# Two experts' weights, one group's keys and a held-back transpose: reordering the loads of a fused attention and mixture-of-experts kernel

## The chip, the cores and the metric

The kernel runs on one core of one Trainium2 chip. The metric is device time in microseconds (us), from launch to the end of the last store; lower is better. A core has a matrix engine (TensorE, "PE" in the profile, its weight loads "PEld"), VectorE (DVE), ScalarE (ACT), GpSimd (POOL) and SyncE (SP). Each engine runs its own instruction stream in order and waits on semaphores. SP issues transfers only; POOL both computes and issues the transfers that cast from fp32 to fp16. Sixteen DMA engines serve all queues.

## The reference

Attention over 4 batches, 8 heads, 768 positions and 64 channels. Three heads (0, 2, 6) use plain causal attention; the five others see only the first 4 positions and a window of 64. The result, 3072 tokens of 512 channels, goes through four experts; every expert sees every token, and their outputs are summed with normalised weights.

```python
scores = scale * np.matmul(q, k.transpose(0, 1, 3, 2))
causal = rel >= 0
stream_keep = causal & (is_sink | in_win)
scores = np.where(mask[None, :, :, :], scores, -1000000000.0)
a = np.exp(scores - np.max(scores, axis=-1, keepdims=True))
attn = np.matmul(a / (np.sum(a, axis=-1, keepdims=True) + 1e-09), v)

x = attn.transpose(0, 2, 1, 3).reshape(3072, 512)
p = domain_probs / (domain_probs.sum(-1, keepdims=True) + 1e-09)
for e in range(4):
    h = np.maximum(x @ w1[e], 0.0)          # 512 -> 1024
    out += p[:, e:e + 1] * (h @ w2[e])      # 1024 -> 512
```

## The kernel before

**Groups.** The tokens are cut into 8 groups of 384 (half a batch each). `attention(b, c)` computes group g = 2b + c into a tile `xT[g]`, channels on partitions. The experts work through tokens in three stages: `plain_steps(0, 3, e, ...)` for each expert e on all of group 0 (three tiles of 128 tokens), `plain_steps(3, 1, e, ...)` on the first tile of group 1, and then `pair_steps` on ten pairs of tiles. Group 0's attention runs alone at the start (`front`, driven by the hand-written string `FRONT`). All later attention is woven into the expert work.

**The weave.** `moe_steps` yields after each few matmuls, with a modelled length and a share; the loop at the end adds them up in `spent` and calls `attention_step` while the planned attention is behind what `due` says. For group 1 `due` interpolates in `FIRST` (L1746): pairs of (expert work done, in units of one expert on group 0; fraction of group 1's attention to be done by then). A unit's layer 1 is weighed with 0.6 and its layer 2 with 1.4. So FIRST decides where in the instruction streams of PE, DVE and ACT group 1's attention stands.

**One unit.** In `plain_steps` layer 1 takes 8 blocks of four matmuls of 384 columns (L1224), each emptied by ACT with a ReLU (L1251). For expert e the first 7, 4, 2 or 2 blocks start with the first half of the contraction (channel tiles 1 and 0, in chunk 0 of w1(e)) and come back for the second half (chunk 2). Layer 2 (L1269) takes six runs of four matmuls of 512 columns, in the order first half of tiles 0 and 1, second half of tiles 0 and 1, tile 2; DVE adds each finished tile to the accumulator (L1286).

**Group 1's attention.** It has no DMA transpose for its inputs: keys and queries arrive as rows (`k16`, `qt16`, by `load_triples`) and `transposes(hp)` turns a pair of heads on PE (L792), the queries into one PSUM buffer, the keys into another. For hp of 0 and 1 both come from `pV`, which has two buffers, and for 2 and 3 from `pA`, which has four and serves scores and layer 1 too. ACT empties the queries (L805, hp below 2), DVE the keys of the even head (L813) and of the odd one (L825). Then `scores(h)` (L893) fills a `pA` bank by tile, ACT takes the exponential (L911), DVE masks (L918, L922), `values` follows (L951 for the three plain heads, L1003 for the others). The plain heads' outputs go to `x_one` (head 0) and `x_pair` (heads 2 and 6), and SP turns each by one DMA transpose into `xT[g]` (L985).

**The loads.** From L575 to L602 POOL's stream holds by hand the casts of the early values, the memsets and the requests for all weights and for group 1's keys, queries and values. w1(e) is four requests (chunk 0 and 2, each for two halves u of the partitions), w2(e) two. `landed(x)` is a copy of one element by POOL into `seen`: POOL waits there until the transfer that wrote x is done. Each POOL request also takes one of eight semaphores in turn, so it waits until the eighth request before it has landed. The early keys, queries and values of group 0 come on the queues of SP and ACT (L454, L437, L439) in fp32, to `k32`, `q32` and `v32`.

Of the kernel before, what the change touches and what calls it, by code (L numbers as in the profile page):

```python
# [12 lines left out]
FP16 = mybir.dt.float16  # L13
# [6 lines left out]
def kernel(  # L20
# [33 lines left out]
    nc = tc.nc  # L54
    P = 128
    B, H, S, D = q.shape
    E, DM, F = moe_w1.shape
# [3 lines left out]
    HP = H // 2  # L61
# [10 lines left out]
    SH = [h for h in range(H) if not RETR[h]]  # L72
# [15 lines left out]
    pers = ctx.enter_context(tc.tile_pool(name="pers", bufs=1))  # L88
# [53 lines left out]
    bS = early[:, 1792:2272].rearrange("p (t x) -> p t x", t=3)  # L142
    eps = pers.tile([P, 1], FP32, name="eps")
    seen = pers.tile([P, 1], FP16, name="seen")[0:1, :]
    mC = pers.tile([P, P], FP16, name="mC")
    mS = pers.tile([P, 4, TQ], FP16, name="mS")
    mW = mS.rearrange("p t x -> p (t x)")[:, 0 : (WT + 2) * WQ].rearrange(
# [22 lines left out]
    def half(u):  # L170
        return slice(u * D, (u + 1) * D)
# [5 lines left out]
    def own_v(h):  # L177
        return half(PLACE[h][1])
# [10 lines left out]
    def v_tiles(b, c, h):  # L189

        if RETR[h]:
            return vR[b % 2][:, 3 * c : 3 * c + 3, RH.index(h), :]
        if b:
            return windows(vSf)[:, :, SH.index(h), :]
        return vS[:, c, :, SH.index(h), :]
# [10 lines left out]
    def rows_of(x, b, h, c):  # L206
        return x[b, h, c * CH : (c + 1) * CH, :].rearrange("(j p) d -> p j d", p=P)

    def tiles_of(x, b, h, c):
        return x[b, h, c * CH : (c + 1) * CH, :].rearrange("(t r) d -> r t d", r=TK)  # L210

    def windows_of(x, b, h, c):

        assert b > 0
        first = ((b * H + h) * S + c * CH - WO) * D
        return bass.AP(x.tensor, x.offset + first, [[D, P], [WQ * D, WT], [1, D]])
# [85 lines left out]
    def load_v(b, c, heads):  # L302
        for h in heads:
            t = v_tiles(b, c, h)
            if RETR[h]:
                gp.dma_start(out=t[:, :, 0:D], in_=rows_of(v, b, h, c))
            elif b:
                gp.dma_start(  # L308
                    out=t[:, :, own_v(h)], in_=windows_of(v, b, h, c)
                )  # L310
            else:
                gp.dma_start(
                    out=t[R0:P, :, own_v(h)],
                    in_=tiles_of(v, b, h, c),
                )
# [7 lines left out]
                out=vS[0:NS, c, t, :, :], in_=vS[R0 : R0 + NS, 0, 0, :, :]  # L323
            )

    def load_w1(e, chunks=(0, 2)):
        x = moe_w1[e].rearrange("(u c d) f -> u d c f", u=2, c=DMP)
        for c in chunks:
            for u in range(2):
                gp.dma_start(  # L330
                    out=w1sb[half(u), e * DMP + c : e * DMP + c + 2, :],
                    in_=x[u, :, c : c + 2, :],
                )

    def in_pairs(e):

        return e < 2
# [11 lines left out]
    def load_w2(e):  # L349
        x = w2sb[:, e * FTP : (e + 1) * FTP, :]  # L350
        for n in range(2):
            if in_pairs(e):
                m = slice(n * FTP // 4, (n + 1) * FTP // 4)
                gp.dma_start(
                    out=x.rearrange("p (m j) d -> p m (j d)", j=2)[:, m, :],
                    in_=moe_w2[e].rearrange("(m p j) d -> p m (j d)", p=P, j=2)[
                        :, m, :
                    ],
                )
                continue  # L360
            m = slice(n * FTP // 2, (n + 1) * FTP // 2)
            gp.dma_start(
                out=x[:, m, :],
                in_=moe_w2[e].rearrange("(fo fi) d -> fi fo d", fi=P)[:, m, :],
            )
# [44 lines left out]
    def rows32(n):  # L410
        x = hA[:, n * 6 * H * D : (n + 1) * 6 * H * D].bitcast(FP32)
        return x.rearrange("p (s x) -> p s x", s=HP)

    q32, k32 = rows32(0), rows32(1)
# [28 lines left out]
    def cast_v(eng, heads):  # L443
        for h in heads:
            if RETR[h]:
                out_, in_ = v_tiles(0, 0, h)[:, :, 0:D], vR32[:, RH.index(h), :, :]
            else:
                out_ = v_tiles(0, 0, h)[:, :, own_v(h)]
                in_ = vS32[:, STAGE.index(h), :, :]
            eng.tensor_copy(out=out_, in_=in_)  # L450
# [8 lines left out]
    for s in (0, 2, 1, 3):  # L459
# [3 lines left out]
            name=nc.get_next_instruction_name(),  # L463
# [14 lines left out]
        out=probs,  # L478
        in_=moe_domain_probs[0 : NPL * P, :].rearrange("(t p) e -> p t e", p=P),
    )  # L480
    nc.sync.dma_start(
        out=p_in.rearrange("t x e -> t (x e)"),
        in_=moe_domain_probs.rearrange("(t x) e -> t (x e)", x=P),
# [77 lines left out]
    qt16 = att.tile([P, H, 3, D], FP16, name="q16", bufs=1)  # L561

    def landed(x):

        gp.tensor_copy(out=seen, in_=x)

    def w1_of(e):
        return w1sb[D : D + 1, (e + 1) * DMP - 1, 0:1]


    def w2_of(e):
        return w2sb[0:1, (e + 1) * FTP - 1, 0:1]


    cast_v(gp, (1,))  # L575
    load_w1(0, (0,))
    cast_v(gp, (5, 4, 0))
    load_w1(0, (2,))
    cast_v(gp, (6, 2, 3, 7))
    load_w2(0)  # L580
# [2 lines left out]
    one_values(gp, 1)  # L583

    load_w1(1)
    landed(w1_of(0))
    load_triples(k, k16, 0, 1, 0, HP)
    load_triples(q, qt16, 0, 1, 0, HP)
    landed(w2_of(0))
    load_w2(1)  # L590
    landed(qt16[0:1, 0, 0, 0:1])
    load_w1(2)
    load_triples(k, k16, 0, 1, HP, H)
    load_triples(q, qt16, 0, 1, HP, H)
    load_v(0, 1, RH)
    landed(w2_of(1))
    load_v(0, 1, SH[:2])
    load_w2(2)
    load_v(0, 1, SH[2:])
    landed(w1_of(2))  # L600
    load_w1(3)
    load_w2(3)  # L602
    assert E == 4
    mSf = mS.rearrange("p t x -> p (t x)")
# [6 lines left out]
    def mm_ns(cols):  # L611
        return cols / 2.4 + 2.5
# [161 lines left out]
    def attention(b, c):  # L774
        g = b * NCH + c
# [155 lines left out]
        def values_r(h):  # L931

            ct, u = PLACE[h]
            shared = by_dma and ct
            if not (shared and u):
                pv_of[0] = pV.tile([P, 512], FP32, name="pV", bufs=2)
            ps = pv_of[0]
            heads = ps.rearrange("p (u x) -> p u x", u=2)[:, :, 0 : 3 * (D + 2)]
            heads = heads.rearrange("p u (j x) -> p u j x", j=3)
            ps = heads[:, u if shared else 0, :, :]  # L940
            work = []

            for es, parts in es_of[h][1:] + es_of[h][:1]:
                for t, o, q0, nq in parts:
                    for j in range(3):
                        x = j * P - q0
                        if 0 <= x < nq:
                            work.append((j, t, es[:, o + x : o + x + P]))
            ns = 0
            for n, (j, t, lhsT) in enumerate(work):  # L950
                nc.tensor.matmul(  # L951
                    out=ps[:, j, 0 : D + 1],
                    lhsT=lhsT,
                    rhs=vR[i][:, t, RH.index(h), 0 : D + 1],
                    start=(n == 0),
                    stop=(n == len(work) - 1),
                    skip_group_check=True,
                )
                ns += mm_ns(D + 1)
                if ns > 200 and n < len(work) - 1:  # L960
                    yield ns
                    ns = 0
            x = x_pair if ct else x_one
            if shared and not u:
                yield ns
                return
            if shared:
                rs = att.tile([P, 2, 3, 1], FP32, name="rs", bufs=2)
                sums, top = heads[:, :, :, D : D + 1], heads[:, :, :, 0:D]
                to = x.rearrange("p j (u d) -> p u j d", u=2)  # L970
                shape = [P, 2, 3, D]
            else:
                rs = att.tile([P, 2, 3, 1], FP32, name="rs", bufs=2)[:, 0, :, :]
                sums, top, to = ps[:, :, D : D + 1], ps[:, :, 0:D], x[:, :, half(u)]
                shape = [P, 3, D]
            nc.vector.tensor_scalar(
                out=rs, in0=sums, scalar1=1e-9, scalar2=None, op0=ALU.add
            )
            nc.vector.reciprocal(out=rs, in_=rs)
            nc.vector.tensor_tensor(  # L980
                out=to, in0=top, in1=rs.to_broadcast(shape), op=ALU.mult
            )
            yield ns
            if h != 2:
                nc.sync.dma_start(  # L985
                    out=xT[g][:, ct, :].rearrange("p (j x) -> p j x", j=3),
                    in_=x.rearrange("p j x -> p (j x)"),
                    transpose=True,
                )
# [753 lines left out]

    first_pair = E * UNIT + ONE

    FIRST = ((1.2, 0.0), (2.0, 0.277), (2.14, 0.277), (2.4, 0.55), (3.3, 1.0))  # L1746
    plan = {1: (FIRST[0][0] * UNIT, FIRST[-1][0] * UNIT)}
    begin = E * UNIT + 0.6 * ONE
    for a, n in zip(range(2, G), (0.72, 1.65, 2.95, 4.15, 5.4, 6.65)):
# [33 lines left out]
    def due(a):  # L1783
        if a == 1:
            for (lo, x), (hi, y) in zip(FIRST, FIRST[1:]):
                if spent <= hi * UNIT:
# [50 lines left out]
```

## Time and profile before

| what | us |
|---|---|
| runs before, three | 373.61, 372.96, 372.58 |
| median of the runs | 372.96 |
| the profiled execution's own time | 373.37 |
| its span | 371.6 |
| busy: PE, DVE, ACT, POOL | 365.0, 279.8, 227.0, 118.7 |
| PE enters expert 1's layer 1 on group 0 | 28.27 |
| PE's first transposes of group 1 | 32.80 |
| PE enters expert 2's layer 1 on group 0 | 42.65 |
| SP issues the transpose of x_one, of x_pair | 50.74, 59.31 |
| PE enters layer 1 on group 1's first tile | 70.23 |

The span is the time from the first to the last instruction on the core; the profiled execution's own time holds 1.8 us more around it. PE's granted clock is full in every slice. A row of a timeline gives start, length, engine, line, operation, tiles, shape, count, and in brackets the idle time of the engine just before the row and what ended it. A matmul's printed end is modelled and lies past the start of the next one, so gaps between rows are better counted from start to start. A DMA's row on POOL or SP is its issue; when it lands stands in the list of issues, as us from issue to landing.

### The profile page before, as it was taken

The page shows a single profiled execution, that of the slowest core. Times are in us where ns is not written, and L with a number is a line of the kernel's source. Part 1 is how long each engine was busy: PE and PEld are TensorE (multiplying, and loading weights), DVE is VectorE, ACT ScalarE, POOL GpSimd, SP SyncE. Part 2 cuts the span into 40 slices and gives each one's busy share as a digit, 9 for nine tenths or more (in the row PEclk, how much of TensorE's full clock was granted, in tenths as well). Part 3 has the DMA queues.
Part 4 walks back from the last instruction along what each step waited for, and adds up shares of the span by engine and source line. Part 5 has one row for each costly group of instructions (what it writes and reads, how often), then busy time and mean ns, then how long its engine had stood idle before and what let it go on. Part 6 is the DMA issues. An engine that isn't in the chain of part 4 may idle for free.

```text
span 371.6 us, 10363 instructions
## 1 busy us (share of the span) xinstructions
PE 365.0 (98%) x4240; PEld 310.4 (84%) x4240; DVE 279.8 (75%) x586; ACT 227.0 (61%) x476; POOL 118.7 (32%) x173
## 2 busy tenths in 40 slices
PE   8999999999999999999999999999999999999996
PEld 5744566578998989999989899998899998998996
DVE  7864785898697589778657849867768868979882
ACT  6735779357777785775776856774777361451630
POOL 6975656784075049026402740220000000000000
PEclk9999999999999999999999999999999999999999
DMA  8999999999999399969906991960220300300101
GB/s 220 176 194 208 174 198 172 188 195 131 125 110 152 87 104 145 141 98 90 175 11 76 157 152 27 127 127 6 73 69 2 114 3 2 116 2 10 50 3 56
DMA packets 119716, 39.65 MB, mean 107 GB/s; under 512 B 107648, under 2 KB 112324, under 8 KB 119668
## 3 DMA queue, kind: packets, MB, share of 16 engines
q0 software_dynamic: 82816, 18.62, 58.8%
q1 hardware_dynamic: 35764, 19.58, 25.2%
q10 hardware_dynamic: 1088, 0.79, 0.7%
q8 instruction: 33, 0.54, 0.6%
q14 instruction: 15, 0.12, 0.1%
HBM read 44.89 MB, written 6.34 MB: 138 GB/s over the span
## 4 chain that ended last, share of the span: by engine, by line
PE 82%; DMA 11%; POOL 4%; DVE 1%; issue 1%; ACT 0%; SPq 0%; POOLq 0%
PE pO L1569 31%; PE pA L1386 23%; PE pO L1415 9%; DMA w1sb<-in_moe_w_dram 5%; PE pA L893 4%; PE pO L1269 3%; PE pA L1224 3%; DMA q<-in_q_dram 2%; PE pV L1415 2%; PE pA L1415 2%; DMA w2sb<-in_moe_w_dram 2%; POOL w1sb L330 2%; PE pV L1003 2%; PE pV L951 2%; DMA hA<-in_v_dram 1%; DMA hA<-in_q_dram 1%
## 5 line engine op out<-in xcount | busy, mean ns | idle before, releaser
L1569 PEld LDWEIGHTS <-hA 128*128 128x128 f16 x1104 | 104.8, 98 | 11.9
L1386 PE MATMUL pA<-xs,w1sb 128*128 128x256 f16 x768 | 97.1, 272 | 0.0
L1386 PEld LDWEIGHTS <-w1sb 128*128 128x128 f16 x768 | 71.7, 98 | 7.3
L1569 PE MATMUL pO<-w2sb,hA 128*128 128x256 f16 x640 | 76.8, 272 | 0.0
L1395 ACT ACTIVATE hA<-pA 128x512 f16<-128x512 f32 x96 | 57.2, 598 | 28.9 <-PE pA L1386 26.6
L911 ACT ACTIVATE es<-pA 128x384 f16<-128x384 f32 (+2 forms) x122 | 58.3, 513 | 25.0 <-PE pA L893 22.1
L308 POOL DMA_DIRECT2D vS<-in_v_dram x30 | 29.6, 988 | 106.6 <-PE pV L1003 106.0
L1569 PE MATMUL pO<-tsb,hA 128*128 128x256 f16 x464 | 56.8, 272 | 0.0
L1334 DVE TENSOR_TENSOR xs<-xT,pB 128x1024 f16<-128x1024 f16 (+1 forms) x49 | 47.5, 987 | 1.9 <-DMA vS<-in_v_dram 1.9
L1152 DVE TENSOR_TENSOR hA<-hA 128x1024 f16<-128x1024 f16 x60 | 39.4, 685 | 0.6 <-PE pO L1569 0.3
L1251 ACT ACTIVATE hA<-pA 128x128 f16<-128x128 f32 (+1 forms) x61 | 20.4, 381 | 20.4 <-PE pA L1224 20.1
L1415 PEld LDWEIGHTS <-w1sb 128*128 128x128 f16 x512 | 31.4, 98 | 1.4 <-issue 0.5
L1224 PE MATMUL pA<-xT,w1sb 128*128 128x128 f16 (+1 forms) x244 | 29.3, 270 | 0.5 <-DMA w1sb<-in_moe_w_dram 0.5
L1269 PE MATMUL pO<-w2sb,hA 128*128 128x512 f16 x120 | 28.6, 379 | 1.1 <-DMA w2sb<-in_moe_w_dram 1.1
L1589 ACT COPY s<-pO 128x256 f32<-128x256 f32 x31 | 11.6, 373 | 27.3 <-PE pO L1569 21.8
L1224 PEld LDWEIGHTS <-w1sb 128*128 128x128 f16 x256 | 19.3, 98 | 9.7 <-issue 1.8
L1024 DVE TENSOR_TENSOR xT<-pV,rc 64x384 f16<-64x384 f32 x35 | 19.4, 555 | 9.5 <-ACT rc L1021 8.9
L1432 DVE CUSTOM_DVE_ANT_0 hA<-pO,s 128x512 f16<-128x512 f32 x26 | 17.7, 688 | 9.8 <-PE pO L1415 8.5
L922 DVE TENSOR_TENSOR es<-es,mS 128x384 f16<-128x384 f16 (+1 forms) x40 | 13.6, 345 | 14.9 <-ACT es L911 14.8
L1425 ACT COPY s<-pO 128x512 f32<-128x512 f32 x39 | 22.7, 587 | 3.2 <-PE pO L1415 3.0
L1018 ACT ACTIVATE rc<-pV,eps 64x384 f32<-64x384 f32 x35 | 20.2, 576 | 6.3 <-PE pV L1003 5.7
L1269 PEld LDWEIGHTS <-hA 128*128 128x128 f16 x128 | 12.1, 98 | 13.6 <-issue 1.6
(189 smaller groups left out, 545.6 us busy)
## 6 DMA issues: line engine op xcount, KB each, us to landing
pB<-p_rows SPq DMA_DIRECT2D x10, 512.0 KB
out_dram<-o SPq DMA_DIRECT2D x19, 256.0 KB
w1sb<-in_moe_w_dram POOLq DMA_DIRECT2D x16, 256.0 KB, 7.2
w2sb<-in_moe_w_dram POOLq DMA_DIRECT2D x8, 512.0 KB, 9.4
vS<-in_v_dram POOLq DMA_DIRECT2D x30, 112.0 KB, 4.8
k_rows<-in_k_dram POOLq DMA_DIRECT2D x18, 128.0 KB, 5.6
q<-in_q_dram POOLq DMA_DIRECT2D x18, 128.0 KB, 6.5
out_dram<-hA SPq DMA_DIRECT2D x4, 256.0 KB
```

What stands on the lines that cost most here:

```text
L308: gp.dma_start(out=t[:, :, own_v(h)], in_=windows_of(v, b, h, c))
L911: nc.scalar.activation(out=es[:, 0:cols], in_=ps[:, 0:cols], func=AF.Exp, scale=SC)
L1152: nc.vector.tensor_tensor(out=out, in0=a, in1=b, op=ALU.subtract)
L1224: nc.tensor.matmul(out=ps[:, 0 : x.shape[2]], lhsT=w1_tile(e, CTS[n], ft), rhs=x[:, CTS[n], :], start=(n == 0), stop=(n == DMP - 1),)
L1251: nc.scalar.activation(out=hs[:, ft, :], in_=ps[:, 0:cols_n], func=AF.Relu)
L1269: nc.tensor.matmul(out=ps_o, lhsT=hs[:, ft, j * P : (j + 1) * P], rhs=w2sb[:, e * FTP + ft, :], start=(ft == 0), stop=(ft == FTP - 1),)
L1334: nc.vector.tensor_tensor(out=o, in0=xin, in1=pb.to_broadcast([P, DMP, n, P]), op=ALU.mult)
L1386: nc.tensor.matmul(out=ps[:, f * PC : (f + 1) * PC], lhsT=w1_tile(e, ct, f0 + f), rhs=xs[:, ct, :], start=(ct == 0), stop=(ct == DMP - 1),)
L1395: nc.scalar.activation(out=blocks[:, b0 : b0 + 2, k0 : k0 + 2, :].rearrange("p t f x -> p f t x"), in_=ps.rearrange("p (f t x) -> p f t x" ...
L1415: nc.tensor.matmul(out=ps[:, f * P : (f + 1) * P], lhsT=w_tile(e, w[:, ct, :], f), rhs=a[:, ct, :], start=(first and f == 0 and ct == 0), ...
L1425: nc.scalar.copy(out=kept[n], in_=ps)
L1569: nc.tensor.matmul(out=ps, lhsT=a[:, k, :], rhs=b(k), start=(first and k == 0), stop=(k == KT - 1), skip_group_check=not first,)
```

## The change

It reorders transfers and moves one attention block; no arithmetic is added or removed.

- The first of w1(0)'s four requests moves ahead of `cast_v(gp, (1,))`, behind a new `landed` on the last of the early keys.
- `landed(w1_of(0))` and `landed(qt16...)` go; w2(1)'s two requests, behind `landed(w2_of(0))`, now stand ahead of group 1's keys and queries of heads 0 to 3; `landed(w1_of(1))` now stands ahead of w1(2).
- Head 3's values move behind w2(2), head 4's behind w1(3).
- SP copies one element of w1(3) to a new tile `seen_by_sp` just ahead of group 1's transpose of `x_one`, so SP waits there until w1(3) has landed.
- FIRST begins at 1.7 units instead of 1.2; its other points stay.

```diff
-    def load_w1(e, chunks=(0, 2)):
+    def load_w1(e, chunks=(0, 2), us=(0, 1)):
...
-            for u in range(2):
+            for u in us:
...
+    landed(k32[0:1, HP - 1, 0:1])
+    load_w1(0, (0,), (0,))
     cast_v(gp, (1,))
-    load_w1(0, (0,))
+    load_w1(0, (0,), (1,))
...
     load_w1(1)
-    landed(w1_of(0))
+    landed(w2_of(0))
+    load_w2(1)
     load_triples(k, k16, 0, 1, 0, HP)
     load_triples(q, qt16, 0, 1, 0, HP)
-    landed(w2_of(0))
-    load_w2(1)
-    landed(qt16[0:1, 0, 0, 0:1])
+    landed(w1_of(1))
     load_w1(2)
...
     landed(w2_of(1))
-    load_v(0, 1, SH[:2])
+    load_v(0, 1, (1,))
     load_w2(2)
-    load_v(0, 1, SH[2:])
+    load_v(0, 1, (3, 5, 7))
     landed(w1_of(2))
     load_w1(3)
+    load_v(0, 1, (4,))
     load_w2(3)
...
             if h != 2:
+                if g == 1 and not ct:
+                    nc.sync.dma_start(out=seen_by_sp, in_=w1_of(E - 1))
                 nc.sync.dma_start(
                     out=xT[g][:, ct, :].rearrange("p (j x) -> p j x", j=3),
...
-    FIRST = ((1.2, 0.0), (2.0, 0.277), (2.14, 0.277), (2.4, 0.55), (3.3, 1.0))
+    FIRST = ((1.7, 0.0), (2.0, 0.277), (2.14, 0.277), (2.4, 0.55), (3.3, 1.0))
```

More of the change, by code (lines that the diff above doesn't have):

```diff
@@ L144 @@
     seen = pers.tile([P, 1], FP16, name="seen")[0:1, :]
+    seen_by_sp = pers.tile([P, 1], FP16, name="seen_by_sp")[0:1, :]
     mC = pers.tile([P, P], FP16, name="mC")
```

## The prediction

> **What bounds the kernel now.** I read the page's header first, then TensorE's own timeline of the first 90 us, then the timelines of POOL, of VectorE (DVE) and ScalarE (ACT) between 33 and 44 us, and of SP.
>
> ```profile
> PE 365.0 (98%) x4240; PEld 310.4 (84%) x4240; DVE 279.8 (75%) x586; ACT 227.0 (61%) x476; POOL 118.7 (32%) x173
> ...
> DMA  8999999999999399969906991960220300300101
> ```
>
> TensorE is busy for 365.0 of 371.6 us, so only its idle time can be won, and what delays its stream is lost in full. The DMA engines are full up to slice 13, so until about 120 us the order of the transfers decides when each lands. TensorE's timeline shows where it waited:
>
> ```profile
> 24.82 1.89 PE L1269 MATMUL pO<-w2sb,hA 128*128 128x512 f16 x8 [0.47 <-DMA w2sb<-in_moe_w_dram]
> ...
> 28.27 1.55 PE L1224 MATMUL pA<-xT,w1sb 128*128 128x384 f16 x8
> 30.11 2.76 PE L1224 MATMUL pA<-xT,w1sb 128*128 128x384 f16 x16 [0.30 <-DMA w1sb<-in_moe_w_dram]
> ...
> 36.62 0.33 PE L792 MATMUL pV<-ident,k 128*64 128x128 f16 x6
> 37.56 1.89 PE L1269 MATMUL pO<-w2sb,hA 128*128 128x512 f16 x8 [0.61 <-DMA w2sb<-in_moe_w_dram]
> ...
> 59.69 0.49 PE L1224 MATMUL pA<-xT,w1sb 128*128 128x384 f16 x2 [0.24 <-DMA w1sb<-in_moe_w_dram]
> ```
>
> These are the only waits of TensorE for weights. The printed ends run past the next start, so I count from start to start. In the chain of waits 8 matmuls of 512 columns take 1.73 us (0.216 each) and 12 of 384 columns 1.95 (0.1625). The true gaps are then 24.82 - 22.46 - 1.73 = 0.63, 30.11 - 28.27 - 1.30 = 0.54, 37.56 - (36.42 + 0.46 for twelve transposes) = 0.68, and 59.69 - 58.64 - 0.65 = 0.40: 2.25 us in all. That is the most that better weight timing can win.
>
> POOL's timeline shows the order of requests:
>
> ```profile
> 9.15 0.47 POOL L450 CAST vS<-hA 128x256 f16<-128x256 f32 x1 [1.95 <-DMA hA<-in_v_dram]
> 9.70 1.36 POOL L330 DMA_DIRECT2D w1sb<-in_moe_w_dram  x2
> 11.04 0.76 POOL L450 CAST vS<-hA 128x256 f16<-128x256 f32 x2
> ...
> 22.22 0.79 POOL L232 DMA_DIRECT2D k<-in_k_dram  x1
> 23.00 0.76 POOL L232 DMA_DIRECT2D q<-in_q_dram  x1
> ...
> 25.35 1.51 POOL L354 DMA_DIRECT2D w2sb<-in_moe_w_dram  x2 [0.27 <-issue]
> ```
>
> The list of DMA issues, asked for narrow stretches, gives issue to landing: last piece of w1(1) 21.43 + 8.6 = 30.0, k +8.8 = 31.0, q 23.00 + 9.1 = 32.1, w2(1) 25.35 + 9.2 = 34.6 and 26.14 + 11.4 = 37.5. Landings follow one another in order of request: k costs 1.0, q 1.1, the two halves of w2(1) together 5.4.
>
> **Part 1, w1(0) sooner.** Row group u=0 of the first chunk is issued behind a `landed` on the last early key triple instead of behind `cast_v(1)`. VectorE's cast of those keys starts at 8.74, just released by that DMA. With the copy (0.18) and the 0.27 of issue time behind a waiting copy, the request starts near 9.2, not 9.70. Then `cast_v(1)` ends near 10.4 and u=1 starts near 10.5, as before (9.70 + 0.75). The next casts of values move by under 0.1 us (11.04 to 11.1); POOL stood idle 1.95 us before 9.15, which hides the copy. So one piece of four is earlier by 0.5. What reaches the end of w2(0) is the bandwidth that lay unused: at 11 to 12 us the DMA engines moved 117 GB/s, against 180 and 190 on either side, at most 0.38 us of work. Bounds 0 and 0.48; I take 0.2 (the dip, half used). All landings, and TensorE at its DMA-bound restart at 30.11, come 0.2 earlier. [...]
>
> **Part 2, w2(1) ahead of k and q.** New landings, all minus the 0.2: w2(1) done at 30.0 + 5.4 = 35.4, q at 35.4 + 2.1 = 37.5. TensorE restarts at 30.11, does 24 matmuls of layer 1 (3.90, to 34.01) and 16 of layer 2, which need w2(1) by 35.74 (its second half): landed 0.3 earlier, so the 0.68 wait goes. If that cover is gone, each late us of w2(1) is paid in full up to 0.68.
>
> **Part 3, FIRST 1.2 to 1.7.** The planner weighs layer 1 with 0.6 and layer 2 with 1.4; 1.7 units fall behind the fourth group of layer 2 of expert 1. The order built from the changed kernel says the same: 24 + 16 matmuls, transposes(0), four matmuls, transposes(1), one score tile, four matmuls, seven score tiles, expert 2. Before, the two transposes lay 3.6 us apart (32.80 and 36.42); now only four matmuls (0.86) lie between. They share two `pV` buffers, and the second use of the key buffer waits for VectorE to empty the first. VectorE's rows:
>
> ```profile
> 33.44 0.80 DVE L813 CAST kR<-pV 64x384 f16<-64x384 f32 x1 [2.11 <-PE pV L792]
> 34.27 0.81 DVE L825 CAST kS<-pV 64x384 f16<-64x384 f32 x1
> ...
> 38.65 1.58 DVE L1286 SCALAR_TENSOR_TENSOR hA<-pO,p_sb,hA 128x512 f32<-128x512 f32 x2
> ```
>
> In the changed order the two L1286 stand ahead of these casts. The second of them starts 0.2 behind the 16th matmul (34.01 + 3.45 = 37.46), at 37.66, and ends at 38.41; the two casts take 1.64 with their gaps: 40.08. Transposes(0) run 37.6 to 38.06, four matmuls to 38.9, the query half of transposes(1) to 39.15; the key half stands still until 40.13. **A wait of 1.0 us, in place of the 0.68.** It ends at 40.39, the first score tile at 40.61, four matmuls at 41.47, the second tile at 41.69. Now ACT's rows:
>
> ```profile
> 39.70 2.45 ACT L911 ACTIVATE es<-pA 128x512 f16<-128x512 f32 x5 [1.85 <-PE pA L893]
> 42.47 1.47 ACT L911 ACTIVATE es<-pA 128x512 f16<-128x512 f32 x3 [0.32 <-PE pA L893]
> ```
>
> An exponential every 0.49. With four `pA` banks the second layer-1 bank of expert 2 waits for the sixth exponential, which before began at 42.47. Now the second begins 0.2 behind its tile, at 41.9; the sixth is four steps on (three of 0.49, and one 0.1 shorter behind the tile of 384 columns), 43.75. TensorE enters expert 2's layer 1 later by 43.75 - 42.47 = 1.28, less the 0.2. Bounds: if the halves of w2(1) land as slowly as the second of w2(2) (42.74 + 6.4, then 43.69 + 8.8: 3.4 apart, 6.6 for two instead of 5.4), transposes(0) slip by 1.2 and this grows by 0.9; if the casts could start right behind the transposes (38.17 instead of 38.44), it shrinks by 0.27.
>
> **Part 4, the held transpose and the moved values.** SP's rows:
>
> ```profile
> 50.74 1.30 SPq L985 DMA_TRANSPOSE xT<-x_one  x1
> 59.31 1.46 SPq L985 DMA_TRANSPOSE xT<-x_pair  x1
> 60.95 0.52 SPq L1311 DMA_DIRECT2D pB<-p_rows  x1
> ```
>
> SP now holds x_one's transpose (issued 50.74) until w1(3) has landed. That expert's last piece took 10.1 us from 49.44, where w1 pieces take 7.2 in the median; without the transpose and one values load (0.35) ahead of it, it lands near 58 or earlier, and TensorE, now later, does not wait: the 0.40 goes. Behind the hold on SP stand x_pair's transpose (59.31), the probabilities (60.95) and the keys' and queries' transposes of group 2 (67.68, which wait for k_rows anyway). x_one is needed at 70.2. Head 3's values land behind w2(2), near 53, and are used at 54.5; head 4's behind w1(3), near 59, used at 62.7: hidden, and each late us would be TensorE's.
>
> **Sum**: -0.2 + 1.28 - 0.40 = +0.68 us. Against the profiled execution 373.37 (span 371.6 and 1.8 around it) that is 374.05; the median of the runs, 372.96, lies 0.41 under it, so 373.6. A measurement of this kernel tells about 0.3%, 1.1 us, from no change: this is a loss inside it.
>
> **Rivals.** *All waits go.* If VectorE empties the key buffer in time and ACT's banks come free, the four waits shrink by 0.2 + 0.68 + 0.40 and expert 2's own 0.23 of waits (42.65 to 45.48 for 16 matmuls): -1.5, 371.5. For it: the weights do land earlier; against it: VectorE's order in the build. Chance 0.24. *The transposes come late.* x_one starts only at 58.2 and x_pair queues behind it. Group 2's third query transpose starts at 74.24, and POOL is released by it only at 83.08: 8.8 us. If one follows the other in full, x_pair lands at 58.2 + 17.6 = 75.8, 4.9 behind its need at 70.9; if they overlap as those six did (15.4 us, 2.6 each), at 69.6, hidden. The middle costs 1.8: 375.4. It decides once w1(3) lands after about 59.5. Chance 0.13, and 0.06 for k and q landing late, near 374.5. *It does little*: w1(0) no sooner, stall hidden in part: 373.0, chance 0.07.
>
> **How the numbers follow.** The forecast has 0.50, its own range 373.1 to 374.6 (0.48 earlier, or q late by 1.2); two fifths of it, 0.21, lie beyond 374.1, where 0.3% ends. Slower: 0.13 + 0.06 + 0.21 = 0.40; faster 0.24; within 0.29 + 0.07 = 0.36. The range 371.7 to 375.1 leaves out half of the faster rival and the worst of the late transposes.
>
> **What would show it.** Right: no wait at the w2 matmuls of expert 1; TensorE's second key transposes of group 1 released by VectorE (kS, the second cast) about 1 us late; ACT's exponentials back to back into expert 2; no wait for w1(3). Wrong: key transposes without idle time, expert 2 starting before 42.6, or TensorE waiting for xT near 70 us.

## The result, and the profile after

The changed kernel takes 373.66 us (median of 21 runs, 372.65 to 374.96) where the kernel before takes 372.88 beside it (21 runs, 372.09 to 374.06): a ratio of 1.0021, with a 95% interval of 1.0012 to 1.0031, 0.4 to 1.2 us. The loss is real, and it is about 0.3% at most. The profiled execution has a span of 372.7 us against 371.6.

Line numbers of the changed kernel are up to 5 higher: L1229 and L1274 are the two layers of the experts, L795 the transposes, L896 the scores, L914 the exponentials, L1291 the gathering of the experts' output. TensorE's timeline of the changed kernel (start, busy time, engine, line, operation, tiles, count, idle time before it and what ended that):

```profile
24.19 1.89 PE L1274 MATMUL pO<-w2sb,hA 128*128 128x512 f16 x8 [0.36 <-DMA w2sb<-in_moe_w_dram]
...
27.64 1.55 PE L1229 MATMUL pA<-xT,w1sb 128*128 128x384 f16 x8
30.42 4.06 PE L1229 MATMUL pA<-xT,w1sb 128*128 128x384 f16 x24 [1.24 <-DMA w1sb<-in_moe_w_dram]
34.32 3.62 PE L1274 MATMUL pO<-w2sb,hA 128*128 128x512 f16 x16
...
38.32 1.04 PE L1274 MATMUL pO<-w2sb,hA 128*128 128x512 f16 x4
39.29 0.36 PE L795 MATMUL pV<-ident,q 128*64 128x128 f16 x6
40.31 0.36 PE L795 MATMUL pV<-ident,k 128*64 128x128 f16 x6 [0.66 <-DVE kS L828]
...
41.70 2.26 PE L896 MATMUL pA<-qT,kR 128*128 128x256 f16 x13
44.12 2.93 PE L1229 MATMUL pA<-xT,w1sb 128*128 128x384 f16 x16 [0.17 <-ACT es L914]
...
60.12 1.14 PE L1229 MATMUL pA<-xT,w1sb 128*128 128x384 f16 x6
```

Read against the four waits of before: expert 1's second layer (34.32, 16 matmuls in one piece) no longer waits for w2(1), and expert 3's first layer (60.12) no longer waits for w1(3). In their place the second key transposes wait for VectorE's cast kS at L828: the query half starts at 39.29, the key half at 40.31, 0.83 more than six transposes take. Expert 2's first layer begins at 44.12; behind the restart at w1(1) that is 13.70 us, where before it was 42.65 - 30.11 = 12.54: 1.16 lost. The restart itself is 0.31 later, and the 0.40 at w1(3) is won: 0.31 + 1.16 - 0.40 = 1.07, and TensorE comes to group 1's first tile 1.08 later (71.31 against 70.23). From there to the end of the span all 14 traces of this document take 301.3 to 301.4 us, so nothing behind that point bears on the result.

VectorE and ScalarE of the changed kernel, in the same stretch:

```profile
37.11 1.61 DVE L1291 SCALAR_TENSOR_TENSOR hA<-pO,p_sb,hA 128x512 f32<-128x512 f32 x2 [6.41 <-PE pO L1274]
38.64 0.78 DVE L816 CAST kR<-pV 64x384 f16<-64x384 f32 x1
39.45 0.80 DVE L828 CAST kS<-pV 64x384 f16<-64x384 f32 x1
40.71 0.79 DVE L816 CAST kR<-pV 64x384 f16<-64x384 f32 x1 [0.46 <-PE pV L795]
```

```profile
41.03 0.60 ACT L914 ACTIVATE es<-pA 128x512 f16<-128x512 f32 x1 [0.32 <-PE pA L896]
42.12 3.32 ACT L914 ACTIVATE es<-pA 128x512 f16<-128x512 f32 x7 [0.48 <-PE pA L896]
```

The two L1291 end at 38.7, the casts that empty the key buffer run 38.64 to 40.25, and the transposes start at 40.31. Then seven exponentials follow one another at 0.47 each and hold the banks that expert 2 wants (from start to start, the last score tiles and expert 2's first two banks wait 0.25 + 0.27 + 0.17 + 0.33 + 0.17).

POOL and SP of the changed kernel:

```profile
8.40 0.37 POOL L566 CAST seen<-hA 1x1 f16<-1x1 f32 x1 [1.21 <-DMA hA<-in_k_dram]
8.72 0.75 POOL L331 DMA_DIRECT2D w1sb<-in_moe_w_dram  x1
9.47 0.41 POOL L451 CAST vS<-hA 128x256 f16<-128x256 f32 x1
9.83 0.59 POOL L331 DMA_DIRECT2D w1sb<-in_moe_w_dram  x1
10.41 0.74 POOL L451 CAST vS<-hA 128x256 f16<-128x256 f32 x2
```

```profile
56.90 0.60 SPq L989 DMA_DIRECT2D seen_by_sp<-w1sb  x1
57.59 1.30 SPq L990 DMA_TRANSPOSE xT<-x_one  x1
60.79 1.19 SPq L990 DMA_TRANSPOSE xT<-x_pair  x1
```

The first request for w1(0) came 0.98 sooner than before (8.72 against 9.70), the second and the casts behind it about 0.6 (10.41 against 11.04 for the next casts). TensorE was 0.49 ahead at its first layer 1 (16.73 against 17.22) and 0.63 ahead after expert 0 (27.64 against 28.27). All of that was lost at w1(1), whose wait grew from 0.54 to 1.48. The hold released the transpose of x_one at 57.59, behind the last piece of w1(3), which landed at 56.88 (59.56 before).

### The profile page after: what moved, and what is told of

Same layout as the page of the kernel before. It is cut to its first block, busy times and chain, and to the rows that moved or that the text cites. A ratio compares the mean times of both kernels' runs of the same rounds, so it can differ in the third digit from the quotient of the medians.

```text
span 372.7 us, 10365 instructions
## 1 busy us (share of the span) xinstructions
PE 365.2 (98%) x4240; PEld 310.3 (83%) x4240; DVE 279.1 (75%) x586; ACT 227.2 (61%) x476; POOL 118.5 (32%) x173
## 4 chain that ended last, share of the span: by engine, by line
PE 89%; DMA 5%; POOL 2%; DVE 2%; ACT 1%; SPq 0%; issue 0%; ACTq 0%
PE pO L1574 31%; PE pA L1391 23%; PE pO L1420 9%; PE pA L1229 6%; PE pO L1274 6%; PE pA L896 5%; DMA w1sb<-in_moe_w_dram 3%; PE pV L1420 2%; PE pA L1420 2%; PE pV L954 2%; PE pV L1008 2%; DMA hA<-in_q_dram 1%; DMA hA<-in_v_dram 1%; DVE xs L1339 1%; ACT es L914 1%; POOL vS L382 1%
## 5 line engine op out<-in xcount | busy, mean ns | idle before, releaser
L1574 PEld LDWEIGHTS <-hA 128*128 128x128 f16 x1104 | 104.9, 98 | 11.9
L914 ACT ACTIVATE es<-pA 128x384 f16<-128x384 f32 (+2 forms) x122 | 58.3, 514 | 23.2 <-PE pA L896 20.8
L1229 PE MATMUL pA<-xT,w1sb 128*128 128x128 f16 (+1 forms) x244 | 29.0, 270 | 1.4 <-DMA w1sb<-in_moe_w_dram 1.2
L1274 PE MATMUL pO<-w2sb,hA 128*128 128x512 f16 x120 | 28.5, 379 | 0.4 <-DMA w2sb<-in_moe_w_dram 0.4
L1229 PEld LDWEIGHTS <-w1sb 128*128 128x128 f16 x256 | 19.5, 98 | 10.6 <-issue 2.3
L896 PE MATMUL pA<-qT,kR 128*128 128x128 f16 (+2 forms) x141 | 23.2, 261 | 0.2
```

Of the source, the lines that this page charges most:

```text
L896: nc.tensor.matmul(out=ps[:, o : o + nq], lhsT=key_tile(b, c, h, t), rhs=qTs[b, c][:, hp, q0 : q0 + nq], start=(n == 0 or not first), stop ...
L914: nc.scalar.activation(out=es[:, 0:cols], in_=ps[:, 0:cols], func=AF.Exp, scale=SC)
L1229: nc.tensor.matmul(out=ps[:, 0 : x.shape[2]], lhsT=w1_tile(e, CTS[n], ft), rhs=x[:, CTS[n], :], start=(n == 0), stop=(n == DMP - 1),)
L1274: nc.tensor.matmul(out=ps_o, lhsT=hs[:, ft, j * P : (j + 1) * P], rhs=w2sb[:, e * FTP + ft, :], start=(ft == 0), stop=(ft == FTP - 1),)
L1574: nc.tensor.matmul(out=ps, lhsT=a[:, k, :], rhs=b(k), start=(first and k == 0), stop=(k == KT - 1), skip_group_check=not first,)
```

## The experiments

Each time is the median of 4 to 12 executions, each ratio is to the kernel before on the same chip, with its 95% interval. The traces show one execution of each kernel. Line numbers shift by a few from kernel to kernel.

### e1: the earlier piece of w1(0) alone

```diff
+    landed(k32[0:1, HP - 1, 0:1])
+    load_w1(0, (0,), (0,))
     cast_v(gp, (1,))
-    load_w1(0, (0,))
+    load_w1(0, (0,), (1,))
```

> The kernel before with the earlier first piece of w1(0) alone. In the changed kernel the values' cast, the second piece and TensorE's first layer 1 all came about 0.5 to 0.6 us sooner (16.73 against 17.22), and nothing of it was left at the last piece of w1(1) (landed 30.29 against 29.98; restart at 30.42 against 30.11). Theory A (the transfers are a stream that is full until 30 us, so that a request issued sooner changes only who lands first): TensorE's first layer 1 starts near 16.7, its wait for w2(0) ends 0.5 sooner, near 24.2, and the restart behind w1(1) stays within 0.3 of 30.1; the time stays within 0.2 of before. Theory B (the sooner request was worth its 0.5, and it was w2(1), asked for right behind w1(1) in the changed kernel, that slowed w1(1)): the restart comes at 29.6 and the time falls by 0.5. Theory C (the sooner request itself costs w1(1) 0.3): restart at 30.4, time up 0.3.

Measured: 372.50 us, ratio 0.9986 (0.9976 to 0.9997), half a microsecond better than before. TensorE's waits for weights in this kernel:

```profile
25.42 1.89 PE L1271 MATMUL pO<-w2sb,hA 128*128 128x512 f16 x8 [0.99 <-DMA w2sb<-in_moe_w_dram]
...
28.87 4.24 PE L1226 MATMUL pA<-xT,w1sb 128*128 128x384 f16 x24
...
37.80 1.89 PE L1271 MATMUL pO<-w2sb,hA 128*128 128x512 f16 x8 [0.64 <-DMA w2sb<-in_moe_w_dram]
```

Here the wait was at w2(0), and hardly any was left at w1(1): its last piece landed at 30.22, and the ninth matmul of that layer, the first that needs it, stands at 30.36, against 30.11 before. The restart fits theory A, the time theory B, and C's loss is out; but theory A's sooner end of the wait for w2(0) (24.2) did not come, it ended at 25.42. POOL's timeline shows why:

```profile
14.66 0.40 POOL L450 CAST vS<-hA 128x256 f16<-128x256 f32 x1 [1.18 <-DMA hA<-in_v_dram]
15.01 1.44 POOL L354 DMA_DIRECT2D w2sb<-in_moe_w_dram  x2
```

Its last cast of the early values waited 1.18 us for these values, so the request for w2(0) left at 15.01, against 14.46 before. One more trace with the sooner piece, e4, shows such a wait of 1.03, two show 0.2 or less, five none, and the five traces without the piece none at that cast. Whether the sooner piece made these values late is not shown. The traced execution took 373.17 us, nearly the slowest of the twelve (371.44 to 373.20), so it does not show the gain. One profile cannot tell which of neighbouring transfers was late because of the change, since these waits trade places.

### e10: the changed kernel without that piece

The edit of e1 taken out of the changed kernel.

> The changed kernel without its first part: w1(0)'s first piece is asked for behind the values' cast, as before. Theory A (the sooner piece is worth what the run made of it alone gave, 0.5): time about 0.5 above the changed kernel, near 374.1, ratio to before near 1.0035. Theory B (the transfers are full until 30 us, the sooner piece only changes who lands first, and the 0.5 came from where the single transfers fell in that kernel): within 0.2 of the changed kernel (373.66); the restart behind w1(1) between 29.7 and 30.4, where the runs with the sooner piece had it.

Measured: 374.07 us, ratio 1.0045 (1.0028 to 1.0063), 0.4 above the changed kernel by medians. That points to theory A, a second time; the two intervals just touch (the changed kernel's ends at 1.0031), so the size is loose. The last piece of w1(1) landed at 30.02 and TensorE took it up at 30.16, no later than with the sooner piece; what stood out was the wait for q:

```profile
38.18 0.36 PE L793 MATMUL pV<-ident,q 128*64 128x128 f16 x6 [0.49 <-DMA q<-in_q_dram]
```

q landed at 38.14, where in the six kernels with the changed order of requests and the sooner piece it landed between 36.61 and 37.78. This is one trace; it suggests that the half microsecond comes out at the end of the full stretch of transfers and not at w1(1).

### e2: FIRST 1.2 to 1.7 alone

```diff
-    FIRST = ((1.2, 0.0), (2.0, 0.277), (2.14, 0.277), (2.4, 0.55), (3.3, 1.0))
+    FIRST = ((1.7, 0.0), (2.0, 0.277), (2.14, 0.277), (2.4, 0.55), (3.3, 1.0))
```

> The kernel before with the point 1.2 to 1.7 alone: the requests stay in their old order. Theory A (my account: the later point by itself puts both transposes four matmuls apart, so TensorE waits about 0.8 to 1.0 us for the key buffer that VectorE empties, and the exponentials then gate the banks of expert 2): the key transposes of the second triple are released by VectorE, and because w2(1) lands at 37.5 as before while its second half is now wanted near 35.9, a wait of 1.3 to 1.8 for w2(1) stands ahead of the transposes; expert 2's layer 1 begins near 44.1 + 1.5 = 45.6, and the time is 2 to 3 us above before, less the wait for w1(3) (0.40). Theory B (the wait at the key transposes came from k and q landing later, not from the order): no wait of TensorE for VectorE at those transposes; only the wait for w2(1) grows, and the time is up by about 1.0 at most.

Measured: 375.78 us, ratio 1.0077 (1.0063 to 1.0091), 2.8 above before. Theory A: the wait at the second key transposes is there although k and q landed at 31.7 at the latest, so it comes from the order of the work. TensorE's waits in this kernel (in total, times, longest):

```profile
PE pO L1269 <- DMA w2sb<-in_moe_w_dram: 1.6, 2, 1.1
PE pV L792 <- DVE kS L825: 0.7, 1, 0.7
PE pA L1224 <- DMA w1sb<-in_moe_w_dram: 0.6, 1, 0.6
```

### e12: w2(1) ahead of the keys and queries alone

```diff
-    landed(w1_of(0))
-    load_triples(k, k16, 0, 1, 0, HP)
-    load_triples(q, qt16, 0, 1, 0, HP)
     landed(w2_of(0))
     load_w2(1)
-    landed(qt16[0:1, 0, 0, 0:1])
+    load_triples(k, k16, 0, 1, 0, HP)
+    load_triples(q, qt16, 0, 1, 0, HP)
+    landed(w1_of(1))
     load_w1(2)
```

> The kernel before with w2(1) asked for ahead of group 1's first keys and queries, the attention left at 1.2. Theory A (the two parts belong together: w2(1) sooner pays only if the attention begins later): no wait for w2(1); but the first key and query transposes, which stand at 32.8, wait for q to land near 37, 4.2 us, of which the second pair, the score tiles and the first half of layer 2 behind them win nothing back: time 3 to 4 us above before, less the 0.68; 375.3 to 376.5. Theory B (the transposes' place matters little since the same weights have to land by 37.5 anyway): within 1.0 of before.

Measured: 379.26 us, ratio 1.0175 (1.0159 to 1.0190): theory A in kind, but 6.4 us and not 3 to 4. TensorE's timeline and, in windows, each engine's busy time with the granted TensorE clock behind it (window, length, the five engines with their counts, clock, DMA share, GB/s):

```profile
28.80 4.43 PE L1223 MATMUL pA<-xT,w1sb 128*128 128x384 f16 x24
38.15 0.53 PE L791 MATMUL pV<-ident,q 128*64 128x128 f16 x6 [4.91 <-DMA q<-in_q_dram]
38.47 0.53 PE L791 MATMUL pV<-ident,k 128*64 128x128 f16 x6
38.93 2.71 PE L1223 MATMUL pA<-xT,w1sb 128*128 128x384 f16 x8
```

```profile
38.00:39.80 1.80, 1.65 (x15) 1.04 (x16) 0.69 (x1) 1.00 (x2) 1.37 (x2) 0.52 1.12 209
39.80:41.40 1.60, 1.60 (x6) 0.76 (x5) 0.91 (x2) 0.49 (x1) 1.07 (x3) 0.50 1.18 199
41.40:44.00 2.60, 2.60 (x23) 1.20 (x22) 0.13 (x1) 0.79 (x2) 1.62 (x3) 0.98 1.76 178
```

The wait for q is 5.08 from start to start, where 4.2 was expected, and behind it the granted clock is 0.50 to 0.52 for 3.3 us (38.15 to 41.46), which the expectation did not have: the twelve transposes take 0.78 instead of 0.46 and the eight matmuls 2.53 instead of 1.30. 5.08 + 0.32 + 1.23, with the wait for w2(1) (0.68) gone and the restart 0.36 later, makes 6.3. The two parts of the change need each other: alone they cost 6.4 and 2.8.

### e3: the second triple's transposes in other buffers

The changed kernel; the second triple takes `pA` banks, as the third and fourth already did.

```diff
-            if hp > 1:
+            if hp > 0:
```

> The changed kernel with one number changed: the second triple's transposes take the buffers that the third and fourth use (pA) and not the pair pV. Theory A (TensorE waits because the key buffer of pV has not yet been emptied by VectorE): the 0.66 that the trace puts on VectorE's cast at those transposes is gone; the first score tile starts up to 0.8 sooner, and as far as the casts and banks behind it let it, expert 2's layer 1 begins 0.3 to 0.8 sooner than 44.12 (the casts of the second triple, 1.6, still stand between the transposes and its own scores); time 0.3 to 0.8 under the changed kernel, near 372.9 to 373.3. Theory B (the wait only stands for the exponentials' pace, which sets expert 2's entry anyway): the wait moves from the transposes to the score banks, expert 2 still begins at 44.1 and the time is that of the changed kernel within 0.2.

Measured: 372.80 us, ratio 0.9995 (0.9983 to 1.0008), 0.86 under the changed kernel.

```profile
38.62 0.36 PE L795 MATMUL pA<-ident,q 128*64 128x128 f16 x6
38.82 0.33 PE L795 MATMUL pA<-ident,k 128*64 128x128 f16 x6
...
41.26 1.17 PE L896 MATMUL pA<-qT,kR 128*128 128x128 f16 x8 [0.21 <-DVE kS L828]
42.60 2.93 PE L1229 MATMUL pA<-xT,w1sb 128*128 128x384 f16 x16 [0.17 <-ACT es L914]
```

The key half follows the query half at once. Expert 2 begins 42.60 - 29.70 = 12.90 behind the restart, 0.80 sooner than in the changed kernel. Theory A, just past its upper end: other buffers for the second triple give back the whole net loss.

### e4 and e8: scores drawn out into expert 2

```diff
-    FIRST = ((1.7, 0.0), (2.0, 0.277), (2.14, 0.277), (2.4, 0.55), (3.3, 1.0))
+    FIRST = ((1.7, 0.0), (2.0, 0.19), (2.14, 0.277), (2.4, 0.55), (3.3, 1.0))
```

e4 is the changed kernel with this, e8 has the edit of e3 as well.

> The changed kernel with the second planner point lowered from 0.277 to 0.19, so that the scores of the first triple are drawn out into expert 2's layer 1 (six matmuls between groups of three score matmuls) and do not stand in one row ahead of it. Theory A (expert 2 enters late because eight exponentials at 0.49 hold its banks): the waits for banks behind the key transposes (0.25 + 0.27 + 0.17 + 0.33 + 0.17 = 1.2) fall to 0.4 or less, the wait of 0.8 to 1.0 at the key transposes stays; time 0.6 to 0.9 under the changed kernel, near 372.8. Theory B (the scores are late anyway and what was not waited for here is waited for at the end of the first triple): the sum of waits between 37 and 50 us is unchanged, time within 0.2 of the changed kernel.

> The changed kernel with both edits, the second triple's transposes in pA and the second planner point at 0.19. With the first edit alone the waits of TensorE between its restart at w1(1) and 50 us were 0.15 for q, 0.37 for VectorE's casts at the scores and 0.84 for banks; with the second alone the wait of 0.70 at the key transposes hid what the spread could win. Theory A (with the key buffer's wait gone, drawing the scores out frees the banks): waits from the restart to 50 us fall to 0.6 or less, time 0.3 to 0.6 under the kernel with the first edit alone (372.8), near 372.4. Theory B (the transposes of the third triple, which take the same four banks, then wait for the drawn-out scores): the waits only move, time 372.6 to 373.2.

Measured: e4 373.89 us, ratio 1.0023 (1.0012 to 1.0034), no gain over the changed kernel; e8 373.66 us, 1.0014 (1.0000 to 1.0029), worse than e3. e4 is theory B: the waits from the restart to 50 us sum to 1.97 (0.36 for q, 0.70 at the key transposes, 0.91 for banks), in the changed kernel to 2.02. e8 is worse than either of its theories had it, 0.86 above e3. Its timeline:

```profile
40.67 0.49 PE L1229 MATMUL pA<-xT,w1sb 128*128 128x384 f16 x2
41.46 0.50 PE L1229 MATMUL pA<-xT,w1sb 128*128 128x384 f16 x2 [0.30 <-DVE kS L828]
42.41 0.49 PE L1229 MATMUL pA<-xT,w1sb 128*128 128x384 f16 x2 [0.45 <-DMA w1sb<-in_moe_w_dram]
```

Expert 2 begins sooner and at once waits for a bank that VectorE's cast must free, and then for the weights of w1(2), whose last piece landed at 42.27. With scores brought into layer 1, layer 1 comes before its weights, so in this trace the transfers are the next bound right behind.

### e5, e6, e7, e9: the hold on SP

```diff
                 if g == 1 and not ct:
                     nc.sync.dma_start(out=seen_by_sp, in_=w1_of(E - 1))
```

e5 is the changed kernel without these lines, e6 the kernel before with them alone, e7 the kernel e1 with them, e9 the kernel e3 without them.

> The changed kernel without the hold of the transpose on SP, all else kept. Theory A (in the changed kernel TensorE comes to w1(3) only at 60.1, and the last piece, which landed at 56.9 with the hold and at 59.6 without it before, is not waited for either way): the last piece of w1(3) lands 1.5 to 2.7 later, no wait of TensorE at 59 to 61, time within 0.2 of the changed kernel (373.66). Theory B (the hold is what took the wait for w1(3) away, as the term of 0.40 in the prediction has it): a wait of 0.3 to 0.5 for w1(3) near 60 and a time 0.4 above the changed kernel. Theory C (the hold costs something by what stands behind it on SP): 0.2 to 0.5 under the changed kernel.

> The kernel before with the hold of the transpose on SP alone. Theory A (the transpose among the weights is what made the last piece of w1(3) late): w1(3) lands near 57 to 58 and not at 59.6, the wait of 0.40 at 59.69 is gone, the time falls by 0.2 to 0.4. Theory B (w1(3) is late because the transfers ahead of it are, which the hold does not touch): the wait stays and the time is that of before within 0.2.

> The kernel before with two parts of the change, the earlier first piece of w1(0) and the hold, and without the two that move w2(1) and the attention. Theory A (the first was worth 0.5 by the run made of it alone, the hold up to 0.4, and the loss lies in the later attention): 0.5 to 0.9 under before, near 372.2, which would be under every kernel so far. Theory B (the two gains are one, or the 0.5 was chance): within 0.3 of before.

> The changed kernel with the second triple's transposes in pA and without the hold on SP. In the run with both (372.8) w1(3) landed at 57.46, the transpose was issued at 58.18 and released VectorE only at 65.96, where the multiplication of the head that shares its rows had been ready 0.9 to 1.0 sooner; TensorE lost only about 0.1 there. Theory A (the hold has turned into a risk: TensorE is sooner by 1.5 and the transpose is not; without the hold w1(3) lands as early, as the run of the changed kernel without it showed, 57.08): VectorE's wait of 2.87 falls to about 1.9, time 0.1 to 0.5 under 372.8. Theory B (the hold is what makes w1(3) land at 57 once TensorE is sooner): a wait for w1(3) of 0.3 or more near 58.6, time 0.2 to 0.5 above 372.8.

Measured: e5 373.59 us, 1.0018 (1.0007 to 1.0029); e6 373.75 us, 1.0019 (1.0002 to 1.0036); e7 373.06 us, 1.0007 (0.9994 to 1.0020); e9 372.96 us, 1.0000 (0.9991 to 1.0009). In e5 the last piece of w1(3) landed at 57.08 without any hold, 0.2 later than with it, and TensorE did not wait: theory A, except that the landing did not move. e9 equals e3 within the measurement: VectorE's wait fell from 2.87 to 1.87, as theory A had it, but in e3 it cost nothing. e6 fell on no theory: the wait for w1(3) is gone, yet the time is 0.7 above before. e7 has the time of its theory B, that of before, but it is 0.56 above e1, from which it differs by the hold alone. (The intervals of e1 and e7 overlap by a little, so the price rests on the two together and on the traces; e6's trace also holds a wait of 0.57 for w2(2) at 49.51, far ahead of the hold.) VectorE and TensorE of e7:

```profile
65.95 0.56 DVE L1029 TENSOR_TENSOR xT<-pV,rc 64x384 f16<-64x384 f32 x1 [3.43 <-DMA xT<-x_one]
```

```profile
68.07 1.89 PE L1274 MATMUL pO<-w2sb,hA 128*128 128x512 f16 x8 [0.54 <-DVE hA L1291]
```

VectorE's last multiplication of group 1 writes a head's 64 rows over rows that x_one's transpose fills with zeros, so it must stand behind that transpose. The transpose was issued at 58.20 and released VectorE at 65.95, 7.8 later; the multiplication had been ready near 64.4 (1.87 behind the end of the one before it, as in the kernel before, e5, e9 and e11, all without the hold). Behind it in VectorE's order stand the two L1291 that empty the banks TensorE needs. e6, with w1(3) later still (landed 58.43, against 57.48 in e7), on SP and VectorE:

```profile
59.14 1.29 SPq L988 DMA_TRANSPOSE xT<-x_one  x1
```

```profile
67.00 0.56 DVE L1027 TENSOR_TENSOR xT<-pV,rc 64x384 f16<-64x384 f32 x1 [4.27 <-PE pO L1272]
```

The trace names TensorE as the releaser here, but the row stands 7.86 behind the issue of the transpose, close to the others (7.75 in e7, 7.78 in e3; in e8, where the trace names ScalarE, 8.66). TensorE then waited:

```profile
69.11 1.89 PE L1272 MATMUL pO<-w2sb,hA 128*128 128x512 f16 x8 [1.38 <-DVE hA L1289]
```

In e3, e7 and e6 the multiplication stood 1.01, 1.56 and 2.40 behind the time at which it was ready, and TensorE lost 0, 0.54 and 1.38: in each case the first microsecond is free. In the changed kernel, TensorE's own delay hides the transpose altogether: issued at 57.59, it would land by the same 7.8 to 8.7 between 65.4 and 66.3 (an estimate), and the multiplication is ready at 66.48 and starts then. That is 0.2 to 1.1 us of slack before VectorE waits at all.

### e11: the earlier piece and the moved values, no hold

The kernel e1 with heads 3 and 4 moved in the list of requests:

```diff
-    load_v(0, 1, SH[:2])
+    load_v(0, 1, (1,))
     load_w2(2)
-    load_v(0, 1, SH[2:])
+    load_v(0, 1, (3, 5, 7))
     landed(w1_of(2))
     load_w1(3)
+    load_v(0, 1, (4,))
```

> The kernel before with w1(0)'s first piece sooner and the values of heads 3 and 4 moved behind w2(2) and w1(3), without the hold and without the moved w2(1) and attention. Theory A (it is the values and the place in the stream, and not the held transpose, that brings w1(3) forward): the last piece of w1(3) lands 0.5 to 1.5 sooner than 59.56, no wait at 59 to 60, and, since x_one's transpose is not held, no wait for VectorE near 68; time 0.5 to 0.9 under before, 372.2 to 372.5. Theory B (the transpose is what delays w1(3)): the wait for w1(3) stays near 0.3, time that of the kernel with the sooner piece alone (0.5 under before) or above it.

Measured: 372.49 us, ratio 0.9989 (0.9979 to 0.9998), 0.4 under before and the same as e1, a little short of theory A's 0.5 to 0.9. Its only wait of TensorE for weights:

```profile
PE pA L1227 <- DMA w1sb<-in_moe_w_dram: 0.7, 1, 0.7
```

w1(3) landed at 56.12, 3.4 sooner than in the kernel before, and was not waited for; the landing of theory A, and more of it. It was not waited for in e1 either (landed 58.73; TensorE began that layer at 58.88 and needs the last piece only behind four matmuls), so the values bring the landing forward, and the time does not show it. Over all 14 traces the last piece of w1(3) landed between 56.09 and 57.67 in the eight kernels with the moved values and between 57.48 and 59.56 in the six without; among the eight, three without the hold have it at 56.09, 56.12 and 57.08. e1 and e11 are the two kernels whose intervals lie below the one before.

## Why the prediction came out

The forecast was 373.6 and the time 373.66. The mechanism named was the one that cost; but the terms of its sum of +0.68 were each off by about 0.2 and made up for one another, so that the sum came this close is luck. The four signs of being right that it named are all in the trace. The table holds, for kernels with the old place of the attention and with the new one, what the traces show (landings from the list of DMA issues; the wait and the last column from start to start, the last one from the restart at w1(1) to expert 2's layer 1):

| kernel | w1(1) landed | w2(1) landed | wait for w2(1) | to expert 2 |
|---|---|---|---|---|
| before | 29.98 | 37.52 | 0.68 | 12.54 |
| e1 | 30.22 | 37.76 | 0.71 | 12.54 |
| e6 | 29.60 | 36.46 | 0.03 | 12.02 |
| e7 | 29.89 | 36.79 | 0.07 | 12.02 |
| e11 | 29.50 | 36.32 | 0 | 12.03 |
| changed | 30.29 | 34.85 | 0 | 13.70 |
| e5 | 29.78 | 34.71 | 0 | 13.71 |
| e3 | 29.57 | 34.42 | 0 | 12.90 |

*Part 1, w1(0) sooner (-0.2).* The term was probably too small: 0.5 (e1, interval 0.1 to 0.9) and 0.4 (e10 against the changed kernel), near the upper bound of 0.48. What failed is the time of the request, "near 9.2" from the cast that VectorE started at 8.74: POOL saw the keys and asked at 8.72, and in the nine traces with the sooner piece at 8.78 in the mean (8.21 to 9.56), against 9.62 in the five without. So in the changed kernel the piece did not push the next casts back either ("near 10.4", "11.1"): they came 0.6 sooner. How the gain arrives stays open. The last piece of w1(1) landed at 29.83 in the mean of nine traces with the sooner piece and 29.89 in five without, each spread over 0.8, so "TensorE at its DMA-bound restart at 30.11, come 0.2 earlier" is not what the traces show. The 0.31 by which the changed kernel's restart was later is within that spread too.

*Part 2, the wait for w2(1) (0.68).* Gone in every trace with the new order, as forecast. What the sum could not see is that the 0.68 was one draw: with w2(1) at its old place among the requests it landed between 36.3 and 37.8 and cost 0.71, 0.07, 0.03 and 0 in the others. e6 is the cleanest of them, since its requests up to there are those of the kernel before: 36.46 against 37.52. There was about 0.3 to win in the mean of the five.

*Part 3, the later attention (+1.28).* Right in kind and size. The wait of 1.0 at the second key transposes came as 0.83, released by the cast named, and the entry of expert 2 moved by 1.16 against the profile of before. Against the mean of the five rows with the old place, 12.23, it is 1.47. e2 shows that the order alone makes the wait at the key transposes, e3 that with other buffers expert 2 comes 0.80 sooner. What is left in e3, 0.88 against the 12.02 of e6 and e7, goes with waits that its trace has there: 0.14 for q, 0.37 for VectorE's casts at the scores and about 0.6 for banks that the exponentials hold; no run takes these away.

*Part 4, the hold and the values (-0.40).* The wait for w1(3) is gone, but the hold was not needed for it: e5 without it has nearly the same landing (57.08) and the same time. The step "without the transpose and one values load (0.35) ahead of it, it lands near 58 or earlier" credited the transpose with what the values, the earlier requests and TensorE's own delay did (e11, with neither hold nor delay, landed at 56.12). Whether the hold has an effect of its own stays open: with it alone w1(3) landed 1.13 and 1.25 sooner (e6 against before, e7 against e1), but e2 and e12, with neither hold nor moved values, have it at 58.34 and 58.44, as e6 does (58.43). And e1 did not wait although its last piece landed only at 58.73, so the 0.40 was a draw as well.

*The rivals.* "The transposes come late" is a true mechanism, named at the wrong reader: "x_one is needed at 70.2" overlooked VectorE's multiplication over the same rows, ready at 64.99 in the kernel before. It costs 0.6 to 0.7 in e7 and e6, and in the changed kernel it misses, by 0.2 to 1.1 us as estimated under e6. "All waits go" did not happen: the two waits in front stayed, and VectorE's order in the build stood against the rest. "It does little" did not come either: its 373.0 lies below the interval of the loss. The sum with the measured terms is about -0.45 (Part 1, between e1 and e10) + 1.47 (Parts 2 and 3 against the mean) - 0.2 (w1(3), the mean of before and e1) = +0.8; 373.66 - 372.88 is 0.78.

## What to carry to other kernels

When work is moved later to give weights the lead, look at what it then stands next to: two uses of one pair of buffers that began 3.6 us apart came within 1.4 (37.87 and 39.29), and the cast between them became the wait; taking other buffers for the second use (e3) gave 0.86 us back. A wait of half a microsecond behind the full stream of transfers was a draw here (0.68, 0.71, 0.07, 0.03 and 0 us for w2(1) at its old place), so read such a wait from several traces before pricing its removal. Before a transfer is held back, list every reader and every writer of its tile, not only the matmul that it is meant for.

## What the hardware showed beside this

Landings in the full stream scatter from kernel to kernel by more than the waits of 0.4 to 0.7 that were to be won: the last piece of w1(1) landed anywhere from 29.50 to 30.34 over 14 traces, and w2(1) at its old place from 36.32 to 37.76 over six. A DMA transpose of 128 x 384 that was issued into the stream of loads took 7.8 us until the write behind it was released (e7: 58.20 to 65.95; e3: 58.18 to 65.96; in e8 8.7, 58.38 to 67.04), about as long as a piece of w1 (7.2 in the median of the kernel before). After TensorE had stood still for 5.1 us in e12, its granted clock was 0.50 to 0.52 for 3.3 us (0.98 in the window behind, 41.4 to 44.0) and the 384-column matmuls took 0.32 instead of 0.16; the wait of 1.48 us in the changed kernel left no such trace (a granted clock of 1.00 from 30.0 to 34.5; the 24 matmuls behind it take 0.1625 each).
